# Three score tiles of 576 neighbouring PSUM columns, filled two tiles ahead

## The chip, the cores and the metric

The kernel runs on one core of one Trainium2 chip. The metric is the device time of one execution in microseconds (us). The core has TensorE (PE: matmuls, with PEld for its weight loads), VectorE (DVE), ScalarE (ACT), GpSimd (POOL), SyncE (SP), whose queue issues all loads, stores and DMA transposes here, and PSUM, the memory that PE writes its products to.

## The reference

Three stages follow one another. First attention with a top-k mask on q, k and v of shape 4 x 8 x 576 x 64:

```
scores = q @ k.T / sqrt(64)
kth = the 32nd largest score of each row
attn = exp(scores - max) where scores >= kth, else 0
attn = attn / (sum(attn) + 1e-9)
x = attn @ v          # heads side by side: 2304 tokens x 512
```

Then two two-layer networks on the 2304 tokens, 512 to 2048 to 512: the first with h * sigmoid(h) between its layers, the second with ELU (h where h > 0, else exp(h) - 1). All inputs are fp32.

## The kernel before

The work is cut into 18 chunks of 128 tokens and each chunk into 8 tiles, 144 tiles in all. A tile is one head's 128 query rows against all 576 keys. As 576 is 4 x 128 + 64, the 64 rows left over of two batches share one chunk, whose tiles hold two heads. The chunks come as batch 0 (4), leftovers of 0 and 1, batch 1 (4), batch 2 (4), leftovers of 2 and 3, batch 3 (4). Values are split into two fp16 halves (hi and lo) so that fp16 matmuls keep fp32 accuracy.

`slot(s)` writes out by hand the order of all instructions of one step of the pipeline; nothing is reordered afterwards, so each engine works through its queue in that order. In slot s stand:

- the scores of tile s+1 (`emit_qk`, L463): 4 matmuls of 288 columns, or 8 for two heads, after the mask of tile s-1, whose buffer they take;
- on DVE the top-k of tiles s and s-1, interleaved: four times MAX8 (the 8 largest of a row, L495) and three times MATCH_REPLACE8 (take them out, L499). The first of each reads the scores in PSUM, the later ones an SBUF copy `r`. After the first MATCH_REPLACE8 comes `bias` (L508), and ACT takes the exponential of the raw scores (L510). Last comes the mask (L523): keep the exponential where the score is at least the 32nd largest, and add the row up. Of tile s the slot holds the first four DVE steps, of tile s-1 the last four. In the order written, the exponential of tile s comes before the mask of tile s-1;
- `emit_ehi(s-1)` on ACT (L549), `emit_elo(s-2)` on POOL (L555, L556) and a DMA transpose into `et` (L558), then `emit_av(s-3)` on PE (L577): exponentials times values. There is one buffer `e16` between them;
- the two networks, 13 and 25 slots behind: `emit_in` (PE, 48 matmuls, L633), `emit_act` (ACT, 3 or 4 instructions), `emit_g` (POOL, L661), `emit_ghi` (ACT, L665), `emit_glo` (POOL), `emit_out` (PE, 12 matmuls of 512 columns, L681). A slot holds one such step. In slots whose number is 2 modulo 8 the attention output of a chunk is taken over (`emit_evac`, `x_hi`, `x_lo`); at the end of slots with 5 modulo 8 the input of the second network is scaled and split on ACT (`x_hi(1, ...)`: the `y` and `x` pieces), and POOL's half follows.

Queries, keys and values must be scaled and split before use. `prep` places these steps: the load, a sum of squares on ACT (`square`), for keys and values a matmul that adds the sums up over partitions (`add_up`, L175, into a spare column of the next score tile), a few one-column instructions on DVE, and the split: `*_hi` on ACT at the end of a slot, `*_lo` (a subtraction, L164) on POOL in the next. For batch 0 the keys come right before use; for batches 1 to 3 keys and values are prepared early, kept in DRAM and fetched later. A reduced sum stands at the end of slot r, its split at the end of slot r+2. Before, r is 17+4i for the keys of pair i of batch 1, 39+8i of batch 2, 73+8i of batch 3, and the values come 2, 4 and 4 slots after. Query sums stand at the end of even slots, query splits at the end of odd ones.

The decoding, scaling and splitting of the networks' weights (DVE, ACT, POOL) goes on through slots -3 to 24.

The score tiles before: two buffers `ps_s`, each of two banks of 512 columns, of which the first 288 hold half of the scores. So every tile has its banks to itself. The changed kernel has one tile object of four banks, and its three tiles of 576 columns follow one another without a gap.

Of the kernel before, what the change touches and what calls it, by code (L numbers as in the profile page):

```python
# [10 lines left out]
F32 = mybir.dt.float32  # L11
# [3 lines left out]
AF = mybir.ActivationFunctionType  # L15
ALU = mybir.AluOpType
AX = mybir.AxisListType.X
PSUM = bass.MemoryType.PSUM
# [13 lines left out]
def kernel(  # L32
# [11 lines left out]
    nc = tc.nc  # L44
    B, H, S, D = q.shape
# [6 lines left out]
    LO = S - SF  # L52
    KR = S // 64
    NC = FC + 1
    HALF = S // 2
    NWP = KFF
    NS = KFF // 4
    NP = H // 2
# [3 lines left out]
    def pool(name, bufs, **kw):  # L62
        return ctx.enter_context(tc.tile_pool(name=name, bufs=bufs, **kw))
# [22 lines left out]
    qs_p = pool("qs", 5)  # L86
    dram = pool("dram", 1, space=bass.MemoryType.DRAM)
    p2_p = pool("p2", 6)
    ps_s = pool("ps_s", 2, space=PSUM)
    ps_h = pool("ps_h", 2, space=PSUM)  # L90
    ps_a = pool("ps_a", 1, space=PSUM)
    ps_v = pool("ps_v", 1, space=PSUM)
# [13 lines left out]
    NTILE = NCH * H  # L106
# [5 lines left out]
    def tile_heads(t):  # L112
        kind, b, c = chunks[t // H]
        j = t % H
        if kind == "f":
            return [(b, j)]
        e, i = LEFT[j]
        return [(b + e, 2 * i), (b + e, 2 * i + 1)]
# [49 lines left out]
    fixed = const.tile([128, 2 + NXS], F32, name="fixed")  # L168
    g1, ones = fixed[:, 0:1], fixed.bitcast(BF16)[:, 2:3]
    due = []  # L170

    def add_up(ps):
        for x, (m, done) in enumerate(due):
            dst = ps[:, 1, HALF + 8 * x:HALF + 8 * x + 1]
            nc.tensor.matmul(out=dst, lhsT=ones.to_broadcast([128, 128]), rhs=m.bitcast(BF16)[:, 1:2], start=True, stop=True)  # L175
            done(dst)
        due.clear()
# [273 lines left out]
    Sps, ets, avs = {}, {}, {}  # L451
    rs_p = pool("rs", 2)

    def emit_qk(t):
        ps = ps_s.tile([128, 2, 512], F32, tag="S", name="S")
        qt = qT[t // 2]
        hs = tile_heads(t)
        n = 128 // len(hs)
        for e, bh in enumerate(hs):
            kt = kT[bh]  # L460
            for p in range(2):
                for a in range(2):
                    nc.tensor.matmul(  # L463
                        out=ps[n * e:n * e + n, a, 0:HALF],
                        lhsT=qt[:, 2 * (t % 2) + p, n * e:n * e + n],
                        rhs=kt[:, a * HALF:(a + 1) * HALF],
                        start=(p == 0),
                        stop=(p == 1),
                    )
        Sps[t] = ps  # L470

    e32s, sums, lsums, cs = {}, {}, {}, {}

# [6 lines left out]
        cs[t] = small.tile([128, 2], F32, tag="c", name="c")  # L480
        pmul(cs[t], qsc[t // 2][:, 2:3].to_broadcast([128, 2]), ik[:, b * NP + h // 2, :])

    def fold(x):
        return x.rearrange("p (a x) -> p a x", a=2)

    def topk_ops(t):
        st = {}
        n = TOPK // 8
        src = Sps[t][:, :, 0:HALF]

        def mx(i):
            if i == 0:
                st["m8"] = small.tile([128, n, 8], F32, tag="m8", name="m8")
                st["r"] = r_p.tile([128, S], F32, tag="r", name="r")
            nc.vector.max(st["m8"][:, i, :], src if i == 0 else st["r"])  # L495

        def mr(i):
            r = st["r"]
            nc.vector.match_replace(  # L499
                out=fold(r) if i == 0 else r,  # L500
                in_to_replace=st["m8"][:, i, :],
                in_values=src if i == 0 else r,
                imm_value=LOW,
            )
            if i == 0:
                c = cs[t]
                bias = small.tile([128, 1], F32, tag="bias", name="bias")
                nc.vector.tensor_scalar(bias, st["m8"][:, 0, 0:1], c[:, 1:2], LN2_14, op0=ALU.mult, op1=ALU.add)  # L508
                e = e32_p.tile([128, S], F32, tag="e32", name="e32")
                nc.scalar.activation(out=fold(e), in_=src, func=AF.Exp, scale=c[:, 0:1], bias=bias)  # L510
                e32s[t] = e

        def mask():
            e = fold(e32s[t])
            ch, j = divmod(t, H)
            if j == 0:
                sums[ch] = rs_p.tile([128, H], F32, tag="sum", name="sum")
                if chunks[ch][0] == "l":
                    lsums[ch] = rs_p.tile([128, H], F32, tag="lsum", name="lsum")
            if chunks[ch][0] == "l":  # L520
                j = LEFT[j][0] * NP + LEFT[j][1]
            acc = lsums.get(ch, sums[ch])[:, j:j + 1]
            nc.vector.scalar_tensor_tensor(  # L523
                e, src, st["m8"][:, n - 1, 7:8], e, op0=ALU.is_ge, op1=ALU.mult, accum_out=acc
            )
            Sps.pop(t)

        ops = []
        for i in range(n):
            ops.append(lambda i=i: mx(i))  # L530
            if i < n - 1:
                ops.append(lambda i=i: mr(i))
        ops.append(mask)
        return ops

# [11 lines left out]
    def emit_ehi(t):  # L547
        h = e16_p.tile([128, 2 * S], F16, tag="e16", name="e16")
        nc.scalar.activation(out=h[:, 0:S], in_=e32s[t], func=AF.Copy)  # L549
        e16s[t] = h  # L550
# [140 lines left out]
    def x2_copy(ch):  # L691
        acc = accs.pop((0, ch))
        y = o_p.tile([128, DM], F32, tag="o", name="y")
        nc.vector.tensor_scalar(y, acc, 1.0, None, op0=ALU.mult)
        z = small.tile([128, 4], F32, tag="z", name="z")
        square(y, z[:, 0:1])
        x2s[ch] = (y, z)
        return z[:, 0:1]
# [38 lines left out]

    KEARLY = 1  # L740
    LDA = -99
    LDB = 28
    LAG = 13
# [8 lines left out]
    loads, sumsq, tiny, early, splits, late, low, decs = (defaultdict(list) for _ in range(8))  # L752

    def prep(slots, load, total, reduce, ops, hi, lo):
        s0, s1, s2 = slots
        if reduce and s1 >= 0:
            s0, s1 = s0 - 1, s1 - 1
        loads[s0].append(load)

        def a():  # L760
            m = total()
            if reduce:
                due.append((m, lambda m: early[s2].append(lambda: ops(m=m))))
            else:
                tiny[s2].append(ops)

        sumsq[s1].append(a)
        late[s2].append((hi, lo))

    first = {b: min(t for (bb, _), t in first_use.items() if bb == b) for b in range(B)}  # L770
    for (b, i), t in first_use.items():
        x = dict(b=b, i=i)
        if b == 0:
            prep((t - 5, t - 4, t - 3), partial(k_load, **x), partial(k_sum, **x), True,
                 partial(k_ops, **x), partial(k_hi, **x), partial(k_lo, **x))
            late[t - 2].append((partial(k_tp, **x), None))
            prep((t - 1, t, t + 1), partial(v_load, **x), partial(v_sum, **x), True,
                 partial(v_ops, **x), partial(v_hi, **x), partial(v_lo, **x))
        else:
            d = 2 if b == 1 else 4  # L780
            r = first[b] - 17 - 8 * (d - 2) + 2 * d * i
            prep((r, r + 1, r + 2), partial(k_load, **x), partial(k_sum, **x), True,
                 partial(k_ops, **x), partial(k_hi, **x), partial(k_keep, **x))
            late[t - 3].append((partial(k_tp, **x), None))
            r += d
            prep((r, r + 1, r + 2), partial(v_load, **x), partial(v_sum, **x), True,
                 partial(v_ops, **x), partial(v_hi, **x, keep=True), partial(v_keep, **x))
            loads[t].append(partial(v_back, **x))
    for g in range(NTILE // 2):
        t = 2 * g  # L790
        prep((t - 5, t - 4, t - 3), partial(q_load, g), partial(q_sum, g), False,
             partial(q_ops, g), partial(q_hi, g), partial(q_lo, g))

    wload, wnow = defaultdict(list), defaultdict(list)
# [31 lines left out]
    for n in range(NWP):  # L826
        x = n, None
# [15 lines left out]
    def slot(s):  # L843
        cur, p1, p2, p5 = (mlp_step(s - x) for x in (0, 1, 2, 5))
        if 0 <= s < NTILE:
            tops[s] = topk_ops(s)
        a = tops.get(s, [])
        b = tops.pop(s - 1, [])
        if due and s < 0:
            add_up(ps_s.tile([128, 2, 512], F32, tag="S", name="S"))  # L850
        summed = [f() for f in early.pop(s, [])]
        small_ops = in_turn(summed + [f() for f in tiny.pop(s, [])])
        pieces = [w_dec_ops(*x, psum=2 <= s < LAG) for x in decs[s]]
# [5 lines left out]
        def dv(*qs, more=True):  # L859
            for o in qs:  # L860
                if o:
                    o.pop(0)()
                if small_ops and (more or s < 0):
                    small_ops.pop(0)()
                for _ in range(per):
                    if dec:
                        dec.pop(0)()
# [21 lines left out]
        if p3 and p3[2] == NS - 1:  # L889
            l, ch, i = p3  # L890
            if l == 0:
                z = x2_copy(ch)
# [12 lines left out]
        t = s - 3  # L905
# [12 lines left out]
        dv(b)  # L918
        if 0 <= s - 1 < NTILE:
            emit_ehi(s - 1)  # L920
        if 0 <= s + 1 < NTILE:
            emit_qk(s + 1)
        if due:
            add_up(Sps[s + 1] if 0 <= s + 1 < NTILE else ps_s.tile([128, 2, 512], F32, tag="S", name="S"))
        dv(a)
        small_ops += in_turn(f() for f in early.pop(s, []) + tiny.pop(s, []) + low[s])
        while small_ops or dec:
# [22 lines left out]
        if s % H == 0 and 0 <= s // H - 1 < NCH:  # L950
            kind, bb, c = chunks[s // H - 1]
# [38 lines left out]
```

## Time and profile before

| | us |
|---|---|
| median of 3 runs | 1188.23 (1186.55 to 1189.44) |
| profiled execution, first to last instruction (span) | 1185.1 |
| PE busy | 940.7 (79%) |
| DVE busy | 1017.0 (86%) |
| ACT busy | 851.7 (72%) |
| POOL busy | 832.6 (70%) |

The page gives no time for what lies around the span. The shares are averages over a first stage, up to about 200 us, in which weights are decoded beside the first tiles, a main stage, up to about 1075 us, in which attention and the networks overlap, and an end, in which only the networks are left. So the stages have to be read one by one.

### The profile page before, as it was taken

How to read it: one execution, taken by the hardware profiler on the slowest of the kernel's cores; microseconds unless marked ns; L12 is line 12 of the kernel's file. 1: busy time of each engine (PE TensorE's matmuls, PEld its weight loads, DVE VectorE, ACT ScalarE, POOL GpSimd, SP SyncE). 2: the span in 40 equal slices, each digit the busy share in tenths (PEclk: the TensorE clock that was granted, in tenths of full speed). 3: DMA queues.
4: the chain of work that ended last, by engine and by line, in shares of the span. 5: the costliest groups of instructions: out<-in, count | busy, mean ns of one | idle time of the engine just before them, and what ended most of it. 6: DMA issues, size and time to landing. Idle time of an engine off the chain costs nothing.

```text
span 1185.1 us, 30883 instructions
## 1 busy us (share of the span) xinstructions
PE 940.7 (79%) x11574; PEld 694.3 (59%) x11574; DVE 1017.0 (86%) x2595; ACT 851.7 (72%) x1663; POOL 832.6 (70%) x1070
## 2 busy tenths in 40 slices
PE   0011112657899999999999989999999999999997
PEld 0000102536666777677767667676777777777765
DVE  6999998997898899999999989999989999995000
ACT  5557556668877788788777778787767777776654
POOL 1148968599777778778776777777776776876543
PEclk9999999878999999999999999999999999999999
DMA  9967473354467646554456545454673444443100
GB/s 307 269 185 225 105 237 87 78 101 102 97 128 122 119 87 119 95 112 100 97 116 133 118 86 110 94 103 104 122 124 67 85 78 82 90 66 65 28 15 14
DMA packets 317318, 132.45 MB, mean 112 GB/s; under 512 B 293488, under 2 KB 300656, under 8 KB 317168
## 3 DMA queue, kind: packets, MB, share of 16 engines
q1 hardware_dynamic: 317168, 130.48, 50.6%
q8 instruction: 91, 1.49, 0.5%
q14 instruction: 59, 0.48, 0.2%
HBM read 52.17 MB, written 12.19 MB: 54 GB/s over the span
## 4 chain that ended last, share of the span: by engine, by line
PE 34%; DVE 20%; POOL 17%; DMA 11%; issue 11%; ACT 5%; SPq 2%; POOLq 0%; ACTq 0%; DVEq 0%
PE a L681 14%; PE h L633 14%; DVE m L495 5%; DMA et<-e 5%; DVE r L499 5%; POOL e L555 4%; POOL gh L164 3%; POOL t L661 3%; PE av L577 3%; PE S L463 3%; DVE W L265 2%; DVE h L262 2%; DVE h L258 2%; DMA W<-in_moe_w_in_dram 2%; DVE e L523 1%
## 5 line engine op out<-in xcount | busy, mean ns | idle before, releaser
L633 PE MATMUL h<-xt,W 128*128 128x128 f16 x6912 | 417.2, 221 | 2.0 <-DMA xt<-x 2.0
L633 PEld LDWEIGHTS <-W 128*128 128x128 f16 x6912 | 402.0, 99 | 14.8 <-issue 4.3
L681 PE MATMUL a<-W,gh 128*128 128x512 f16 x1728 | 401.3, 381 | 9.7 <-POOL gh L164 8.8
L495 DVE MAX8 m<-r 128x8 f32<-128x576 f32 x432 | 312.7, 749 | 1.2
L555 POOL TENSOR_TENSOR e<-e,e 128x512 f16<-128x512 f32 x144 | 167.1, 1160 | 171.5 <-ACT e L549 169.1
L681 PEld LDWEIGHTS <-gh 128*128 128x128 f16 x1728 | 158.9, 98 | 187.4 <-POOL gh L164 16.4
L463 PE MATMUL S<-kt,qt 128*128 128x288 f16 (+1 forms) x640 | 102.8, 304 | 183.4 <-DVE e L523 88.2
L164 POOL TENSOR_TENSOR gh<-t,gh 128x512 f16<-128x512 f32 x144 | 167.0, 1160 | 68.7 <-ACT gh L665 66.2
L499 DVE MATCH_REPLACE8 r<-m,r 128x576 f32<-128x576 f32 x288 | 213.9, 743 | 0.0
L661 POOL TENSOR_TENSOR t<-u,t 128x512 f32<-128x512 f32 x144 | 183.0, 1271 | 30.0 <-ACT u L655 24.6
L463 PEld LDWEIGHTS <-qt 128*128 128x128 f16 (+1 forms) x640 | 56.7, 103 | 241.0 <-issue 104.4
L665 ACT ACTIVATE gh<-t 128x512 f16<-128x512 f32 x144 | 90.2, 626 | 128.2 <-POOL t L661 127.8
L510 ACT ACTIVATE e<-S,bias,c 128x576 f32<-128x576 f32 x144 | 118.0, 819 | 55.6 <-DVE bias L508 50.1
L549 ACT ACTIVATE e<-e 128x576 f16<-128x576 f32 x144 | 97.4, 676 | 62.2 <-DVE p L133 19.1
L495 DVE MAX8 m<-S 128x8 f32<-128x576 f32 x144 | 109.0, 757 | 24.2 <-PE S L463 23.5
L577 PE MATMUL av<-vt,et 128*128 128x64 f16 (+1 forms) x2240 | 95.2, 198 | 26.2 <-DMA et<-e 25.8
L523 DVE SCALAR_TENSOR_TENSOR e<-S,m,e 128x576 f32<-128x576 f32 x144 | 115.4, 802 | 0.5 <-ACT e L510 0.4
L499 DVE MATCH_REPLACE8 r<-m,S 128x576 f32<-128x576 f32 x144 | 107.6, 747 | 0.0
L577 PEld LDWEIGHTS <-et 128*128 128x128 f16 (+1 forms) x2240 | 83.2, 104 | 34.4 <-DMA et<-e 31.4
L164 POOL TENSOR_TENSOR W<-W 128x512 f16<-128x512 f32 x64 | 74.0, 1156 | 5.4
L655 ACT ACTIVATE u<-u,c 128x512 f32<-128x512 f32 x72 | 58.6, 814 | 2.4
L652 ACT ACTIVATE u<-h,c 128x512 f32<-128x512 f32 x72 | 48.4, 673 | 12.4 <-PE h L633 12.4
(108 smaller groups left out, 1134.4 us busy)
## 6 DMA issues: line engine op xcount, KB each, us to landing
W<-in_moe_w_in_dram SPq DMA_DIRECT2D x32, 512.0 KB, 6.6
W<-in_moe_w_out_dram SPq DMA_DIRECT2D x25, 512.0 KB, 5.5
kn<-in_k_dram SPq DMA_DIRECT2D x16, 288.0 KB, 3.1
qn<-in_q_dram SPq DMA_DIRECT2D x64, 64.0 KB, 2.6
out_dram<-o SPq DMA_DIRECT2D x16, 256.0 KB, 2.7
vd<-v SPq DMA_DIRECT2D x12, 320.0 KB, 3.3
vt<-vd SPq DMA_DIRECT2D x24, 160.0 KB, 3.0
kd<-k SPq DMA_DIRECT2D x12, 288.0 KB, 2.2
```

The lines of the kernel that those rows point to most:

```text
L164: nc.gpsimd.tensor_tensor(dst, x, hi, op=ALU.subtract)
L463: nc.tensor.matmul(out=ps[n * e:n * e + n, a, 0:HALF], lhsT=qt[:, 2 * (t % 2) + p, n * e:n * e + n], rhs=kt[:, a * HALF:(a + 1) * HALF], s ...
L495: nc.vector.max(st["m8"][:, i, :], src if i == 0 else st["r"])
L499: nc.vector.match_replace(out=fold(r) if i == 0 else r, in_to_replace=st["m8"][:, i, :], in_values=src if i == 0 else r, imm_value=LOW,)
L510: nc.scalar.activation(out=fold(e), in_=src, func=AF.Exp, scale=c[:, 0:1], bias=bias)
L523: nc.vector.scalar_tensor_tensor(e, src, st["m8"][:, n - 1, 7:8], e, op0=ALU.is_ge, op1=ALU.mult, accum_out=acc)
L549: nc.scalar.activation(out=h[:, 0:S], in_=e32s[t], func=AF.Copy)
L555: nc.gpsimd.tensor_tensor(h[:, S + LO:2 * S], e[:, 0:SF], h[:, 0:SF], op=ALU.subtract)
L577: nc.tensor.matmul(out=o, lhsT=et[:, c, n * e:n * e + n], rhs=r, start=(i == 0), stop=(i == len(seq) - 1))
L633: nc.tensor.matmul(out=ps[:, f:f + 128], lhsT=w, rhs=xt[:, z, :], start=(kk == 0 and x == 0), stop=(kk == KDM - 1 and x == 2),)
L661: nc.gpsimd.tensor_tensor(t, u, t, op=ALU.add if l else ALU.mult)
L681: nc.tensor.matmul(out=acc, lhsT=gh[:, z, u * 128:(u + 1) * 128], rhs=W[:, n, w * 512:(w + 1) * 512], start=(m == 0 and x == 0), stop=(m = ...
```

## The change

One PSUM tile `scores` of four banks is made once. Tile t uses the 576 columns from 576 * (t mod 3); its matmuls are cut where a 512-column bank ends, as 512+64, 448+128 or 384+192. The spare columns of `add_up` come behind the three tiles, from 1728 on. The scores of tile s+2 are written in slot s, where those of s+1 were, after the mask of tile s-1 as before. Queries, and the keys of batch 0, are prepared one slot earlier. The later keys and values have r = 18+4i (batch 1), 37+8i (batch 2) and 73+8i (batch 3), and the keys are brought back one slot earlier (`k_tp`). Query sums then stand at the end of odd slots, query splits at the end of even ones. The first slot is -5 in place of -4. DVE and ACT read a flat run of 576 columns in place of two runs of 288.

```diff
-    ps_s = pool("ps_s", 2, space=PSUM)
+    ps_s = pool("ps_s", 1, space=PSUM)
...
-    def add_up(ps):
+    SB = 3
+    scores = ps_s.tile([128, 4 * 512], F32, name="S")
+
+    def add_up(s):
         for x, (m, done) in enumerate(due):
-            dst = ps[:, 1, HALF + 8 * x:HALF + 8 * x + 1]
+            y = SB * S + 128 * (s % 2) + 8 * x
+            dst = scores[:, y:y + 1]
...
     def emit_qk(t):
-        ps = ps_s.tile([128, 2, 512], F32, tag="S", name="S")
+        x0 = S * (t % SB)
+        cut = 512 * (x0 // 512 + 1) - x0
...
-                for a in range(2):
+                for a, z in ((0, cut), (cut, S)):
                     nc.tensor.matmul(
-                        out=ps[n * e:n * e + n, a, 0:HALF],
+                        out=scores[n * e:n * e + n, x0 + a:x0 + z],
                         lhsT=qt[:, 2 * (t % 2) + p, n * e:n * e + n],
-                        rhs=kt[:, a * HALF:(a + 1) * HALF],
+                        rhs=kt[:, a:z],
...
-        Sps[t] = ps
+        Sps[t] = scores[:, x0:x0 + S]
...
-        src = Sps[t][:, :, 0:HALF]
+        src = Sps[t]
...
-    KEARLY = 1
+    AHEAD = SB - 1
...
         if b == 0:
-            prep((t - 5, t - 4, t - 3), partial(k_load, **x), partial(k_sum, **x), True,
+            y = t - AHEAD
+            prep((y - 4, y - 3, y - 2), partial(k_load, **x), partial(k_sum, **x), True,
                  partial(k_ops, **x), partial(k_hi, **x), partial(k_lo, **x))
-            late[t - 2].append((partial(k_tp, **x), None))
+            late[y - 1].append((partial(k_tp, **x), None))
...
             d = 2 if b == 1 else 4
-            r = first[b] - 17 - 8 * (d - 2) + 2 * d * i
+            r = first[b] - 35 + 2 * d * i + (19 if b == 1 else 2 * (b % 2))
...
-            late[t - 3].append((partial(k_tp, **x), None))
+            late[t - AHEAD - 2].append((partial(k_tp, **x), None))
...
     for g in range(NTILE // 2):
-        t = 2 * g
-        prep((t - 5, t - 4, t - 3), partial(q_load, g), partial(q_sum, g), False,
+        t = 2 * g - AHEAD
+        prep((t - 4, t - 3, t - 2), partial(q_load, g), partial(q_sum, g), False,
...
-        if 0 <= s + 1 < NTILE:
-            emit_qk(s + 1)
+        if 0 <= s + AHEAD < NTILE:
+            emit_qk(s + AHEAD)
         if due:
-            add_up(Sps[s + 1] if 0 <= s + 1 < NTILE else ps_s.tile([128, 2, 512], F32, tag="S", name="S"))
+            add_up(s + 1)
```

## Rows read from the trace of the kernel before

**Rows 1.** Busy time by stretch: stretch, length, PE, PEld, DVE, ACT, POOL, clock, DMA.
```profile
0.00:30.00 30.00, 2.73 (x12) 1.52 (x12) 19.42 (x48) 15.98 (x42) 5.87 (x12) 1.00 0.93 307
...
226.00:290.00 64.00, 44.03 (x476) 31.47 (x472) 56.80 (x155) 45.72 (x89) 60.88 (x80) 0.81 0.46 94
290.00:440.00 150.00, 144.00 (x1834) 105.00 (x1831) 136.36 (x365) 117.91 (x229) 112.40 (x152) 0.99 0.59 115
440.00:665.00 225.00, 213.30 (x2681) 158.98 (x2679) 213.69 (x564) 179.02 (x346) 168.89 (x217) 1.00 0.55 108
665.00:840.00 175.00, 165.16 (x2079) 121.80 (x2077) 163.18 (x430) 139.76 (x270) 131.09 (x171) 1.00 0.52 104
840.00:1075.00 235.00, 235.00 (x3022) 176.11 (x3019) 228.87 (x579) 179.65 (x336) 173.74 (x229) 1.00 0.48 87
```

**Rows 2.** Order of time, PE, around 570 us: start, length, instructions merged.
```profile
567.81 0.65 PE L463 MATMUL S<-kt,qt 128*128 128x288 f16 x4
568.30 2.84 PE L633 MATMUL h<-xt,W 128*128 128x128 f16 x48
570.98 0.57 PE L577 MATMUL av<-vt,et 128*128 128x64 f16 x14
571.39 2.75 PE L681 MATMUL a<-W,gh 128*128 128x512 f16 x12
573.98 0.65 PE L463 MATMUL S<-kt,qt 128*128 128x288 f16 x4
```

**Rows 3.** Waits from 290 to 840 us: who, for whom: us, times, longest.
```profile
ACT gh L665 <- POOL t L661: 67.4, 44, 2.3
...
PE av L577 <- DMA et<-e: 19.6, 17, 3.0
DVE m L495 <- PE S L463: 14.5, 18, 2.0
```

**Rows 4.** Order of time, DVE, from 755 to 762 us.
```profile
756.04 0.77 DVE L495 MAX8 m<-S 128x8 f32<-128x576 f32 x1 [0.20 <-PE S L463]
...
758.18 0.20 DVE L508 TENSOR_SCALAR bias<-m,c 128x1 f32<-128x1 f32 x1
758.30 1.41 DVE L495 MAX8 m<-r 128x8 f32<-128x576 f32 x2
759.63 0.80 DVE L523 SCALAR_TENSOR_TENSOR e<-S,m,e 128x576 f32<-128x576 f32 x1
```

**Rows 5.** Order of time, ACT, before the exponential of tile 94.
```profile
762.15 0.74 ACT L158 ACTIVATE sq<-vn 128x640 fp8e4<-128x640 f32 x1 [0.86 <-DMA vn<-in_v_dram]
...
762.88 0.39 ACT L161 ACTIVATE qn<-qn,qs 128x128 f32<-128x128 f32 x1
763.30 0.42 ACT L440 ACTIVATE q<-qn 128x256 f16<-128x256 f32 x1
763.62 0.70 ACT L161 ACTIVATE y<-y,z 128x512 f32<-128x512 f32 x1
764.36 0.63 ACT L602 ACTIVATE x<-y 128x512 f16<-128x512 f32 x1
764.90 0.81 ACT L510 ACTIVATE e<-S,bias,c 128x576 f32<-128x576 f32 x1
```

**Rows 6.** Order of time, ACT, around the exponential of tile 26.
```profile
302.74 0.81 ACT L161 ACTIVATE vn<-vn,sv 128x640 f32<-128x640 f32 x1
303.59 0.74 ACT L411 ACTIVATE v<-vn 128x640 f16<-128x640 f32 x1
...
304.97 0.81 ACT L510 ACTIVATE e<-S,bias,c 128x576 f32<-128x576 f32 x1
```

**Rows 7.** Order of time, DVE: the mask of tile 25.
```profile
303.61 0.81 DVE L523 SCALAR_TENSOR_TENSOR e<-S,m,e 128x576 f32<-128x576 f32 x1
```

**Rows 8.** Order of time, ACT: the exponential of tile 142.
```profile
1070.22 0.81 ACT L510 ACTIVATE e<-S,bias,c 128x576 f32<-128x576 f32 x1
```

**Rows 9.** Order of time, DVE: the mask of tile 141.
```profile
1069.71 0.80 DVE L523 SCALAR_TENSOR_TENSOR e<-S,m,e 128x576 f32<-128x576 f32 x1
```

More of the change, by code (lines that the diff above doesn't have):

```diff
@@ L54 @@
     NC = FC + 1
-    HALF = S // 2
     NWP = KFF
@@ L481, in emit_c @@
         pmul(cs[t], qsc[t // 2][:, 2:3].to_broadcast([128, 2]), ik[:, b * NP + h // 2, :])
-    def fold(x):
-        return x.rearrange("p (a x) -> p a x", a=2)
     def topk_ops(t):
@@ L499, in mr @@
             nc.vector.match_replace(
-                out=fold(r) if i == 0 else r,
+                out=r,
                 in_to_replace=st["m8"][:, i, :],
@@ L509, in mr @@
                 e = e32_p.tile([128, S], F32, tag="e32", name="e32")
-                nc.scalar.activation(out=fold(e), in_=src, func=AF.Exp, scale=c[:, 0:1], bias=bias)
+                nc.scalar.activation(out=e, in_=src, func=AF.Exp, scale=c[:, 0:1], bias=bias)
                 e32s[t] = e
         def mask():
-            e = fold(e32s[t])
+            e = e32s[t]
             ch, j = divmod(t, H)
@@ L849, in slot @@
         if due and s < 0:
-            add_up(ps_s.tile([128, 2, 512], F32, tag="S", name="S"))
+            add_up(s)
         summed = [f() for f in early.pop(s, [])]
```

## The prediction

> **What bounds the kernel now.** I first read busy time by stretch [rows 1]. Up to 30 us VectorE (DVE) works 19.4 us and waits for the first loads. From 226 to 290 us GpSimd (POOL) is the full engine, 60.9 of 64 us. From 290 us on, TensorE (PE) leads: it is idle for 150 - 144.0 = 6.0, 225 - 213.3 = 11.7 and 175 - 165.2 = 9.8 us, 27.5 us together up to 840 us, and for nothing from 840 to 1075 us. DVE is close behind: 36.8 us idle from 290 to 840, 6.1 us from 840 to 1075.
>
> Next, the order of time of PE around 570 us [rows 2]: from one score group to the next, 567.81 to 573.98, is 6.17 us with nothing idle. That is the least a slot of the main stage can take. From 290 to 840 us there are 84 slots, 6.5 us each, so the whole stage could give back at most the 27.5 us, and the stage after 840 us nothing.
>
> Then the waits of 290 to 840 us [rows 3]. PE stands still mainly because `et`, the transposed exponentials, is late (19.6 us in 17 waits). That chain is mask (DVE), `emit_ehi` (ScalarE, ACT), `emit_elo` (POOL), DMA, `emit_av` (PE). DVE waits for scores 14.5 us in 18 waits. But PE idles little beside it, so those DVE waits are mostly DVE keeping pace with PE. ACT waits 67.4 us in 44 waits for POOL before `gh`, 1.5 us each, which is slack that a later exponential may use.
>
> Last, one slot in detail [rows 4, 5]. The bias of tile 94 ends at 758.38, yet ACT takes its exponential at 764.90, because before it stand a sum of squares of `vn`, the `qn`/`q` pieces and the `y`/`x` pieces of the end of slot 93. DVE ran the mask of tile 93 at 759.63 meanwhile. So DVE is ahead of ACT here by over 5 us.
>
> **The change part by part.**
>
> *Two tiles ahead.* The scores of tile s+2 go where tile s-1 lay, so their matmuls stand at the same place of PE's queue and wait for the same mask(s-1) as those of s+1 do now. What is new is that the scores are wanted one slot later. This removes at most DVE's 14.5 us of waits. While PE is the fuller engine, DVE then only runs ahead and waits elsewhere. Ends: 0 and -14.5; I take 0, since PE's queue sets the slot.
>
> *Pieces of 512+64, 448+128, 384+192 for 288+288.* Same 576 columns, same count of matmuls. The `av` group does 14 matmuls of 64 columns, each with weights of its own, in 571.39 - 570.98 = 0.41 us, 29 ns each [rows 2], so a short piece costs its columns and the edit is 0. The other end: a short piece costs as much as 288 columns do, 0.12 us; beside 512 columns at 2.59 / 12 = 0.216 us this is 2 x 0.336 - 0.49 = 0.18 us a tile, 0.18 x 119 = +21 us after 290 us. Below zero is excluded by the equal columns. I take 0, the row of that size. Flat instead of folded reads by DVE: 0.77 us from the score tile against 1.41 / 2 = 0.70 from a flat tile [rows 4], at most -0.07 a read, on an engine that isn't first: 0.
>
> *Neighbouring columns.* Tiles 0 and 1 of the three now lie together in the columns 512 to 1023, tiles 1 and 2 in 1024 to 1535. Until now every tile had its 512-column banks to itself, so no row shows whether order inside one tile object is kept by column or by bank. If by column, nothing is added. If by bank, two waits come:
> 1. mask(s-1) on DVE waits for exponential(s) on ACT when s mod 3 is 1 or 2. Queued behind the mask on DVE are the rest of top-k(s), all of tile s+1, and on PE the scores of s+2.
> 2. The first max of s+1 waits for the scores of s+2 in two of three slots, at the very place where it waits for PE today, so the first edit's gain shrinks to a third.
>
> I take the bank. In these sentences alone the Trainium skill is weighed: "PSUM — Partial Sum Buffer", section "PSUM bank collisions raise a hardware error", says that no two of TensorE, ScalarE and VectorE may be in one bank and 32-partition quadrant at one time, two readers included, so each such pair has to be ordered. By it the second wait list holds and the term below is paid; by columns alone it would be 0. No row of this trace shows it.
>
> Price of wait 1: how far the exponential's end lies behind the mask's start, for tiles 25 to 143 with s mod 3 not 0, from 305.78 - 303.61 = 2.17 us [rows 6, 7] to 1071.03 - 1069.71 = 1.3 us [rows 8, 9], 57 of 80 tiles above zero, sum 113 us. That is the far end (+113, every wait paid anew). But DVE needs to fall behind only once: after that the exponentials of ordinary slots lie before the mask by themselves. What can be paid again is the rise from one slot to the next beyond the 1.5 us that ACT spends waiting for POOL. Over tiles 25 to 105 that is 16 rises, 25 us in all; from tile 106 on next to nothing (0.2 us), because no key or value is prepared there. Part of the 25 lands where PE would idle for `et` anyway. I take +8, with the next edit counted in.
>
> *Preparation shifted.* Query pieces leave the odd slots' ends for the even ones. Those of batch 2 go from slots 39, 41, 43, 45 + 8i (key sum, key split, value sum, value split) to 37, 39, 41, 43; batch 1 moves one slot later, batch 3 stays. Before, the end of slot 5 of 8 in batch 2 held the value split (304.33 - 302.74 = 1.59 us, [rows 6]), the query split (763.62 - 762.88 = 0.74) and the `y`/`x` pieces (764.90 - 763.62 = 1.28) [rows 5]: 3.6 us before one exponential. After, it holds a key sum (about the 0.73 us of the `vn` one), a query sum (0.4, estimated from the 0.39 of `qn`) and `y`/`x`: 2.4 us. POOL's query subtraction likewise leaves the slots in which it subtracts `x`. The slots in which `et` comes late get lighter in all three batches. Nothing is added in work or DMAs; the SP queue issues the same loads one slot apart. Ends: 0 and all 27.5 us of PE's idle time; a negative effect is possible where batch 1 still meets the query split (4 keys, 4 values, 0.74 us each: +6). I take half of the idle time, -13: the heaviest end of slot loses 1.2 of its 3.6 us, and the pieces that stay still come before an exponential.
>
> *Start.* One more slot of loads, and tile 0 is prepared before the first weights land. DVE has 30 - 19.4 = 10.6 us idle there [rows 1]. Loads of four weights now stand behind the first key transposes in the SP queue. Ends -4 and +4; I take -1. The stage up to 226 us is filled by the same DVE work. From 226 to 290 us POOL's sum stays but for one key's subtraction that leaves it (-1.4 at best); I take 0.
>
> Sum: 0 + 0 + 8 - 13 - 1 = -6 us on the span of 1185.1 us, 1179 us. The page gives no time around that span; the three timed runs lie 1.5 to 4.3 us above it, their median 3.1, and I carry that over: 1182 us.
>
> **The rivals.**
> *Bank waits decide (slower).* DVE stops at mask(s-1) for the exponential of the heavy slots, PE stops behind it at the scores of s+2, and ACT's next exponential then waits for DVE's bias. For it: DVE is only 37 us of 550 short of full, so what it loses it can't make up, and the overlap goes to 6 us in single slots. Against: the lead need be given up only once. If the 25 us of rises are paid in full and half as much returns in the slots after them, with the lighter slots giving back 13 of it, the sum is about 25 + 12 - 13 - 1 = +23. The case lies between 0 and that, its middle at 1188 + 12 = 1200. It decides once the rises are worth over 14 us.
> *Nothing nets.* Waits added and slots lightened cancel, or `et` is late through its DMA, which is unmoved: 1188 us.
> *Columns only, DVE freed.* No wait is added and DVE may run a slot ahead: -13, and up to 6 more of the idle time: 1188 - 18 = 1170. That the change then frees more is barred by PE's 6.17 us.
>
> **How the numbers follow.** Forecast 45%, bank waits decide 30%, nothing nets 18%, columns only 7%. 0.2% is 2.4 us, about what can be told from no change. Faster: 43 of the 45 (the rest within 2.4 us) and 7, 50%; within: 18 and 2, less 1 that falls on the slower side, 19%; slower: 31%. The forecast's own range is 1174 to 1187. The range for 8 in 10 reaches from the columns-only case, 1166, past the middle of the slower case to 1203.
>
> **What would show it.** Right: PE idle 290 to 840 us about 14 us less for `et`; "DVE e <- ACT e" (mask waiting for the exponential) as a new wait, of some tens of us at most, in two of three slots; exponentials starting within 0.1 us of their bias more often. Wrong: no such wait (columns), then a shorter time; or PE's score group waiting for the mask by several us in slots 4 and 6 of 8, then a longer one; or PE's slot longer than 6.17 us from 840 us on, which would be the price of the short pieces.

## The result and the profile after

The changed kernel takes 1200.83 us (median of 4 runs, 1200.39 to 1202.79) against 1187.39 us for the kernel before in the same series: ratio 1.0122, 95% interval 1.0105 to 1.0139. It is 1.2% slower. The profiled execution's span is 1199.1 us, 14.0 us more than before.

Busy time by stretch of the changed kernel, with the columns of [rows 1]:

```profile
226.00:290.00 64.00, 43.34 (x481) 30.77 (x480) 57.32 (x155) 46.23 (x90) 61.88 (x82) 0.84 0.46 96
290.00:440.00 150.00, 139.04 (x1786) 101.46 (x1784) 131.52 (x354) 117.76 (x227) 110.88 (x150) 0.99 0.59 114
440.00:665.00 225.00, 210.77 (x2619) 154.37 (x2618) 208.78 (x551) 179.61 (x343) 167.09 (x215) 0.99 0.55 106
665.00:840.00 175.00, 162.32 (x2014) 119.41 (x2012) 158.82 (x423) 136.32 (x260) 127.48 (x163) 0.98 0.50 100
840.00:1075.00 235.00, 232.80 (x2972) 170.04 (x2971) 225.15 (x568) 174.25 (x328) 168.03 (x223) 1.00 0.49 87
```

PE is now idle for 11.0, 14.2 and 12.7 us in the three stretches from 290 to 840 us, 37.9 us together against 27.5 [rows 1], and for 2.2 us after 840, where it was never idle. DVE idles more too: 50.9 us against 36.8. So no engine has taken PE's place; the engines wait for each other more.

The waits of the changed kernel from 290 to 840 us, with the columns of [rows 3]:

```profile
DVE e L523 <- ACT e L510: 44.5, 25, 4.2
ACT e L510 <- DVE bias L508: 42.9, 42, 2.2
PE S L466 <- DVE e L523: 37.5, 34, 3.8
ACT gh L665 <- POOL t L661: 21.7, 29, 1.8
ACT sq L157 <- DMA vn<-in_v_dram: 17.0, 9, 3.1
ACT sq L157 <- DMA qn<-in_q_dram: 9.8, 11, 1.8
...
DVE m L495 <- PE S L466: 3.6, 6, 1.4
...
PE av L577 <- DMA et<-e: 0.3, 1, 0.3
```

PE's waits for `et` are gone (19.6 us before [rows 3]), and so is most of DVE's waiting for scores (14.5). Both are outweighed by a new chain: the mask waits for the exponential of the next tile (44.5 us), and the next scores wait for that mask (37.5). ACT now often waits for DVE's `bias` (42.9 us in 42 waits, against 4.0 in 4 before), which it did not need to while DVE ran ahead.

One such place in full. The order of time of ACT before the exponential of tile 86 (715.39), with the idle time before a row and what ended it in brackets:

```profile
709.60 0.68 ACT L549 ACTIVATE e<-e 128x576 f16<-128x576 f32 x1
712.95 0.74 ACT L157 ACTIVATE sq<-vn 128x640 fp8e4<-128x640 f32 x1 [2.67 <-DMA vn<-in_v_dram]
713.59 0.19 ACT L157 ACTIVATION_READ_ACCUMULATOR sq<-vn 128x1 f32 x1
713.81 0.31 ACT L157 ACTIVATE sq<-qn 128x128 fp8e4<-128x128 f32 x1
...
714.11 0.70 ACT L160 ACTIVATE y<-y,z 128x512 f32<-128x512 f32 x1
714.85 0.63 ACT L602 ACTIVATE x<-y 128x512 f16<-128x512 f32 x1
715.39 0.81 ACT L510 ACTIVATE e<-S,bias,c 128x576 f32<-128x576 f32 x1
```

The same on DVE: the bias of tile 86, and the mask of tile 85 at 716.23:

```profile
710.97 0.21 DVE L508 TENSOR_SCALAR bias<-m,c 128x1 f32<-128x1 f32 x1
711.09 1.42 DVE L495 MAX8 m<-r 128x8 f32<-128x576 f32 x2
716.23 0.82 DVE L523 SCALAR_TENSOR_TENSOR e<-S,m,e 128x576 f32<-128x576 f32 x1 [3.73 <-ACT e L510]
```

And on PE: the scores of tile 87 (cut 512+64) and of tile 88 (448+128):

```profile
707.57 0.65 PE L466 MATMUL S<-kt,qt 128*128 128x512 f16 x4
708.05 2.84 PE L633 MATMUL h<-xt,W 128*128 128x128 f16 x48
...
711.14 2.75 PE L681 MATMUL a<-W,gh 128*128 128x512 f16 x12
717.11 0.65 PE L466 MATMUL S<-kt,qt 128*128 128x448 f16 x4 [3.21 <-DVE e L523]
717.60 0.17 PE L177 MATMUL S<-mv,fixed 128*128 128x1 bf16 x1
717.63 2.84 PE L633 MATMUL h<-xt,W 128*128 128x128 f16 x48
```

The bias of tile 86 ends at 711.18, so its exponential needs nothing more from then on. But in ACT's queue a sum of squares stands ahead of it, and ACT stands idle for 2.67 us until the values for that sum have arrived. Behind that sum stand a query's, the `y` and `x` pieces, then the exponential, 4.2 us after the bias. DVE's mask of tile 85 waits 3.73 us for it, PE's scores of tile 88 wait 3.21 us for the mask. Before, DVE wrote that mask without looking at the exponential [rows 4, 5]. The score groups themselves take 708.05 - 707.57 = 0.48 and 717.60 - 717.11 = 0.49 us; 288+288 took 0.49 [rows 2].

The mask of tile 77, DVE in order of time, shows the same wait at a tile for which the prediction expected none, since 78 mod 3 is 0 and the tiles 77 and 78 have no bank in common:

```profile
660.42 0.82 DVE L523 SCALAR_TENSOR_TENSOR e<-S,m,e 128x576 f32<-128x576 f32 x1 [3.79 <-ACT e L510]
```

SP's queue ahead of that stall at 712.95 (SPq rows are issues, not transfers):

```profile
705.93 1.29 SPq L558 DMA_TRANSPOSE et<-e  x1
707.27 0.63 SPq L318 DMA_DIRECT2D vn<-in_v_dram  x1
...
709.25 0.59 SPq L328 DMA_DIRECT2D qn<-in_q_dram  x1
```

The loads stand behind the transpose that is issued in their slot, and are issued one after the other; the sums that need them are at the end of the same slot (712.95 and 713.81).

### The profile page after: what moved, and what is told of

It reads as the page before. It is cut to its first block, busy times and chain, and to the rows that moved or that the text cites. A ratio compares the mean times of both kernels' runs of the same rounds, so it can differ in the third digit from the quotient of the medians.

```text
span 1199.1 us, 30805 instructions
## 1 busy us (share of the span) xinstructions
PE 943.3 (79%) x11574; PEld 687.7 (57%) x11574; DVE 1016.0 (85%) x2595; ACT 857.0 (71%) x1663; POOL 833.6 (70%) x1070
## 4 chain that ended last, share of the span: by engine, by line
POOL 23%; DVE 21%; PE 16%; issue 16%; DMA 14%; ACT 7%; SPq 3%; POOLq 0%; ACTq 0%; DVEq 0%
PE h L633 8%; DMA et<-e 6%; PE a L681 6%; POOL t L661 6%; DVE m L495 5%; POOL e L555 5%; DVE r L499 5%; POOL gh L163 4%; DVE e L523 2%; DVE W L267 2%; DVE h L264 2%; DVE h L260 2%; DMA qn<-in_q_dram 2%; POOL e L556 2%; DMA W<-in_moe_w_in_dram 2%
## 5 line engine op out<-in xcount | busy, mean ns | idle before, releaser
L633 PE MATMUL h<-xt,W 128*128 128x128 f16 x6912 | 421.7, 223 | 2.0 <-DMA xt<-x 2.0
L466 PE MATMUL S<-kt,qt 128*128 128x512 f16 (+10 forms) x640 | 103.7, 305 | 229.4 <-DVE e L523 211.6
L466 PEld LDWEIGHTS <-qt 128*128 128x128 f16 (+1 forms) x640 | 52.7, 104 | 294.2 <-issue 232.9
L549 ACT ACTIVATE e<-e 128x576 f16<-128x576 f32 x144 | 97.5, 677 | 69.0 <-DMA et<-e 20.6
```

The lines of the kernel that those rows point to most:

```text
L466: nc.tensor.matmul(out=scores[n * e:n * e + n, x0 + a:x0 + z], lhsT=qt[:, 2 * (t % 2) + p, n * e:n * e + n], rhs=kt[:, a:z], start=(p == 0 ...
L633: nc.tensor.matmul(out=ps[:, f:f + 128], lhsT=w, rhs=xt[:, z, :], start=(kk == 0 and x == 0), stop=(kk == KDM - 1 and x == 2),)
```

## The experiments

All ratios are to the kernel before on the same chip, five rounds, with the 95% interval. Two new orders are at stake, the places of the preparation and the order in the score tiles, and each was tried alone. "Loads early" below means that `prep`'s loads from slot 14 on are issued one slot earlier, and nothing else.

**The preparation alone, on the kernel before** (two banks a tile, one tile ahead; the diff has its core, and batch 0's keys and `k_tp` move one slot earlier too).

```diff
-            r = first[b] - 17 - 8 * (d - 2) + 2 * d * i
+            r = first[b] - 35 + 2 * d * i + (19 if b == 1 else 2 * (b % 2))
...
-        prep((t - 5, t - 4, t - 3), partial(q_load, g), partial(q_sum, g), False,
+        prep((t - 6, t - 5, t - 4), partial(q_load, g), partial(q_sum, g), False,
```

> The kernel before with only the new places of preparation (queries and batch-0 keys one slot earlier, batches 1 to 3 as changed, keys brought back one slot earlier); two score tiles with banks of their own, scores one tile ahead. Theory 1 (the mask's new wait for the next tile's exponential costs, the lighter slots give back): ratio to before 0.99 to 0.998, no wait of the mask for ScalarE, TensorE's waits for et down from 20 us to under 10. Theory 2 (the shifted preparation itself costs): 1.008 to 1.015. Theory 3 (the two-ahead scores and cut matmuls cost): 0.998 to 1.002.

Measured 1.0116 (1.0097 to 1.0134), inside the range of theory 2. On the kernel before, the new places cost 13.8 us where the prediction had them give 13. But this is not quite the term of the change: with scores one tile ahead a key tile is here held one slot longer, while in the changed kernel its scores come a slot earlier too.

**The order alone**: both score tiles of the kernel before in one tile object, each with its own two banks as before.

```diff
+    both = ps_s.tile([128, 2, 2, 512], F32, name="S")
...
-        ps = ps_s.tile([128, 2, 512], F32, tag="S", name="S")
+        ps = both[:, t % 2]
```

> The kernel before, with its two score tiles made as one tile object of four banks; each tile keeps its own two banks, nothing else changes. It adds only the order between the exponential of tile s and the mask of tile s-1, in every slot. Theory 1: slower, 1.010 to 1.025, since the heavy slots are the old ones; the mask waits over 40 us in all for ScalarE. Theories 2 and 3: 0.998 to 1.003.

Measured 1.0101 (1.0085 to 1.0117), 12 us. Its waits from 290 to 840 us:

```profile
DVE e L524 <- ACT e L511: 39.6, 22, 4.8
PE S L464 <- DVE e L524: 29.3, 26, 4.2
```

No two tiles share a bank here, yet the mask waits for the next tile's exponential. So two tiles of one object are ordered even where they have no bank in common. In the changed kernel that order does not stop at the slots with a shared bank either, as the row at 660.42 shows.

Part of this price is paid in TensorE's clock. From the mask of tile 24 to that of tile 104, with the columns of [rows 1], the kernel before and then one object:

```profile
296.85:833.59 536.74, 509.66 (x6423) 376.42 (x6421) 501.57 (x1326) 425.77 (x819) 401.95 (x523) 1.00 0.55 108
297.10:844.90 547.80, 516.35 (x6420) 383.69 (x6418) 500.27 (x1326) 429.72 (x823) 403.16 (x523) 0.98 0.53 107
```

Of the 11.1 us by which this stretch is longer, PE stands idle for 4.4, and 6.7 go to its matmuls, as many as before, at a mean granted clock of 0.98 in place of 1.00. The longest stall shows how:

```profile
664.50 1.12 PE L464 MATMUL S<-kt,qt 128*128 128x288 f16 x4 [4.23 <-DVE e L524]
665.48 4.91 PE L634 MATMUL h<-xt,W 128*128 128x128 f16 x48
```

Behind it 48 matmuls take 4.91 us, against 2.84 in [rows 2]; from 665 to 670 us the granted clock is 0.51, the lower of its two levels (1.2 GHz). In the changed kernel the same stretch has 10.4 us more of idle PE and 2.4 us more of matmuls than in the kernel before.

**Both together, on the kernel before.**

> Both edits of the two runs above together: one tile object of four banks and the new places of preparation, scores still one tile ahead, matmuls still 288 and 288. Theory 1: within 0.3% of the changed kernel, 1.009 to 1.015. Theory 2: the same 1.008 to 1.015, but then one_object alone is at 1.000. Theory 3: 1.000.

Measured 1.0245 (1.0225 to 1.0264), above both ranges: the two losses add up, 1.0116 x 1.0101 = 1.0218, and a little more. The changed kernel is 1.2% better than this.

**The exponential written later in the changed kernel**, behind `emit_ehi(s-1)`, meant to put the mask ahead of it.

```diff
-                nc.scalar.activation(out=e, in_=src, func=AF.Exp, scale=c[:, 0:1], bias=bias)
+                exps[t] = lambda: nc.scalar.activation(out=e, in_=src, func=AF.Exp, scale=c[:, 0:1], bias=bias)
...
+        if s in exps:
+            exps.pop(s)()
```

> The changed kernel with the exponential of tile s written behind the mask and the fp16 copy of tile s-1, so that the mask never waits for it; instead the first max of s+1 and the scores of s+2 wait for it. Theory 1: most of the 55 us of mask waits go and return in part as waits of TensorE and of the first max: 0.995 to 1.006. Theories 2 and 3: 1.010 to 1.014, as the changed kernel.

Measured 1.0737 (1.0718 to 1.0757), a miss of every expectation. The mask's wait went, but the one object orders other pairs in the score tiles as well. From 290 to 840 us:

```profile
PE S L466 <- ACT e L510: 60.7, 73, 2.5
DVE m L495 <- PE S L466: 24.9, 26, 1.6
```

The scores two tiles on now wait for the later exponential, and the first max of the next tile for those scores.

**The new places without the keys' earlier return, and split in two**: all new places of queries and later keys and values (qr_same_ktp), the keys' and values' alone (r_only), the queries' alone (q_only). Their edits are the lines of the first diff.

> The kernel before with queries prepared one slot earlier and the changed places of batches 1 to 3, but the keys brought back where they were, so that no key tile is held a slot longer. If the 1.2% of prep_only came from holding key tiles longer (a ninth buffer of nine in the leftover chunks): 0.996 to 1.003. If the shifted places themselves cost: 1.008 to 1.013. If the lighter slots give what was forecast: 0.985 to 0.992.

> The kernel before with the changed places of keys and values of batches 1 to 3 alone; their loads stay apart from the queries' in batches 2 and 3 and leave the query slots' neighbours in batch 1. If meeting loads are the cause: 0.997 to 1.003. If the places of keys and values were what cost in qr_same_ktp: 1.004 to 1.009.

> The kernel before with queries alone prepared one slot earlier: their loads move from even slots to odd ones, where the loads of the later keys and values stand too. If loads that meet in one slot hold ScalarE's sums and with them the slot: 1.003 to 1.009, ScalarE's waits for loads up from 29 us to 35 to 45. If the new places of keys and values were what cost in qr_same_ktp: 0.997 to 1.002.

Measured 1.0068 (1.0047 to 1.0088), 1.0005 (0.9992 to 1.0017) and 1.0103 (1.0081 to 1.0126). So the queries' shift costs the 1%, the other places are free, and the two together cost 0.7%, which lies in none of the three ranges for it. In batch 1 the new places of r_only bring key and value loads into the queries' slots (both even), so loads in one slot do not cost by that alone. The first experiment's other 0.5% goes with what it had besides: the keys brought back a slot earlier, or batch 0's keys prepared a slot earlier. No run parts these two. From 290 to 840 us, with the queries shifted alone:

```profile
DVE p L133 <- ACT sq L158: 32.6, 15, 4.6
...
PE av L577 <- DMA et<-e: 27.6, 20, 5.4
```

and one of those waits in order of time, the sum of a value on ACT and then DVE:

```profile
767.64 0.74 ACT L158 ACTIVATE sq<-vn 128x640 fp8e4<-128x640 f32 x1 [0.96 <-DMA vn<-in_v_dram]
...
768.93 0.15 DVE L133 TENSOR_SCALAR p<-qs 128x1 int32<-128x1 int32 x1 [2.65 <-ACT sq L158]
```

The one-column instruction `p` stands in DVE's queue ahead of the rest of the top-k and waits for ACT's sum of the query. That sum stands behind the value's, which had waited 0.96 us for its load and takes 0.74 itself; the fp16 copy ahead of both (L549) had waited 1.43 us for a transpose, so the load is about 1 of the 2.65 us. So even where no mask waits for ACT, a late load stops DVE.

**The changed kernel with the old `r`.**

> The changed kernel with the places of keys and values of batches 1 to 3 as before; queries and the two-ahead scores stay changed. If the new places lighten the slots: slower than the changed kernel, 1.015 to 1.022. If they cost: 1.000 to 1.008. If they do nothing: 1.010 to 1.014.

Measured 1.0164 (1.0142 to 1.0185), in the range for places that lighten the slots: going back makes it worse by 0.4%. The new `r` is not what is wrong.

**Loads early**, in the changed kernel, in the kernel before, in qr_same_ktp and in one_object:

```diff
-        loads[s0].append(load)
+        loads[s0 - 1 if s0 >= 14 else s0].append(load)
```

> The changed kernel with the loads of keys, values and queries issued one slot earlier from slot 14 on; nothing else. ScalarE's waits for the value load (about 21 us, at the end of the slot whose next exponential the mask waits 3.7 to 4.1 us for) should go. If the mask's wait takes its length from what ScalarE does and waits for before the exponential: 1.003 to 1.009, mask waits under 45 us. If the order alone costs, whatever its length: 1.011 to 1.014.

> The kernel before with the same earlier loads. There the mask doesn't wait for ScalarE, so only et comes earlier: 0.993 to 1.000. If the same share goes as in the changed kernel (the loads cost by themselves): 0.990 to 0.995.

> qr_same_ktp with all loads one slot earlier from slot 14 on. If its 0.7% is ScalarE waiting for loads: 0.986 to 0.993, level with or below the kernel before with the same earlier loads (0.991). If it is the order of the work itself: 0.997 to 1.001.

> one_object (the mask's new wait alone, old places) with all loads one slot earlier. If the wait's price is ScalarE held by loads before the exponential: 0.991 to 0.997. If the order costs by itself, with the sums and splits alone: 1.000 to 1.005.

| | loads as they were | loads early |
|---|---|---|
| kernel before | 1 | 0.991 (0.9894 to 0.9926) |
| new places, keys' return as before | 1.0068 | **0.981 (0.979 to 0.9829)** |
| one object | 1.0101 | 0.9968 (0.9953 to 0.9984) |
| changed kernel | 1.0122 | 0.991 (0.9897 to 0.9923) |

With the loads early the sign of the new places turns: 0.981 / 0.991 = 0.990, a gain of 1.0% or 12 us. The one object then costs 0.9968 / 0.991, 0.6% in place of 1.0%. The changed kernel gains 2.1% and comes out below both of its ranges; the kernel before gains 0.9%, in its second range; the new places with early loads come out below both of theirs. The best version is the kernel before with the new places and early loads: 1163.59 us, faster than both kernels. Its busy time, columns as in [rows 1]:

```profile
290.00:840.00 550.00, 536.43 (x6812) 397.60 (x6809) 526.65 (x1396) 452.50 (x869) 425.49 (x557) 1.00 0.58 112
840.00:1075.00 235.00, 234.24 (x2992) 175.92 (x2991) 215.13 (x538) 173.32 (x323) 170.98 (x221) 1.00 0.45 81
```

PE idles 13.6 us from 290 to 840 us, against 27.5 before [rows 1] and 37.9 in the changed kernel. The waits of the changed kernel with early loads, same stretch:

```profile
DVE e L523 <- ACT e L510: 21.6, 22, 2.8
PE S L466 <- DVE e L523: 17.4, 32, 2.4
```

The new chain is halved, not gone. No sum waits for a load any more, so what stays is put down to ACT's own work ahead of the exponential.

**Query load and sum ahead of the key's or value's in their slot**, with the queries' shift alone and in the changed kernel:

```diff
-        loads[s0].append(load)
+        loads[s0].insert(len(loads[s0]) if reduce else 0, load)
```

(and the same for `sumsq[s1]`).

> q_only with the query's load and its sum of squares ahead of the key's or value's where both stand in one slot. If the 1.0% of q_only is VectorE waiting for a query sum queued behind a value sum that waits for its load: 0.995 to 1.003, VectorE's waits for the sums under 12 us (32.6 in q_only). If it is the loads meeting in the DMA queues: 1.007 to 1.012.

> The changed kernel with the same: query loads and sums first. Here the exponential, too, stands behind the value sum, and the mask waits for it, so taking the query out of that queue alone should give less: 1.006 to 1.012. If the query queue was the whole loss: 0.995 to 1.001. If the meeting loads: 1.011 to 1.014.

Measured 1.0099 (1.0082 to 1.0117) and 1.0123 (1.0105 to 1.014), no change: the place inside the slot is not it. Both lie in the ranges for loads that meet in the DMA queues, but the transfers themselves are hardly slower: a query load of 64 KB takes 2.6 us from issue to landing (median, 290 to 1075 us) in the kernel before and 2.8 with the queries shifted, a value load of 160 KB 3.2 and 3.5. From 290 to 1075 us of the first:

```profile
DVE p L133 <- PE S L175: 14.0, 12, 3.6
...
DVE p L133 <- ACT sq L158: 10.4, 8, 2.9
```

DVE's wait for query sums fell from 32.6 to 10.4 us, but the key and value sums are now behind, and DVE's wait for them (by way of PE's matmul of L175) rose from 4.2 to 14.0. PE's waits for `et` fell only from 31.2 to 24.9 us. Which load is late changed; that one of them is late did not.

**One kind of load early**: keys and values alone (`reduce and s0 >= 14`), queries alone (`not reduce and s0 >= 14`), each in the changed kernel and with the queries' shift alone.

> The changed kernel with the key and value loads of slots from 14 on issued one slot earlier, and the query loads left where they are. Theory A (ScalarE is held by the key and value loads, the 2.67 us before the vn sum, and everything behind it): most of the gain of all loads early (0.991 to the kernel before) stands, 0.992 to 0.997. Theory B (it is the query loads, which the change put into the slots of the key and value loads): 1.005 to 1.012.

> The changed kernel with the query loads alone one slot earlier. Theory A (key and value loads hold ScalarE): 1.008 to 1.014, the sums of the values still wait for their loads some 17 us in all. Theory B (query loads): 0.992 to 1.000.

> The kernel before with the query preparation one slot earlier, and the key and value loads alone one slot earlier. Theory A (key and value loads hold ScalarE where the query sums stand behind them): the loss of 1.0% goes and the gain of early loads comes, 0.985 to 0.995. Theory B (query loads): 1.003 to 1.010.

> The kernel before with the query preparation one slot earlier and its loads one slot earlier still; keys and values as before. Theory A: the loss stays, 1.006 to 1.011. Theory B: the loss goes, 0.995 to 1.002.

Measured 0.996 (0.9945 to 0.9975) and 1.0044 (1.0027 to 1.0062) in the changed kernel, 0.9927 (0.991 to 0.9944) and 0.9956 (0.994 to 0.9972) with the queries' shift alone. Neither theory holds by itself: two runs fall in a range of A, one in a range of B, and 1.0044 in neither. Both kinds of load hold ACT: in the changed kernel the keys' and values' loads alone give back 1.6% and the queries' alone 0.8%, all together 2.1%; with the queries' shift alone either move takes the whole loss away. Set beside ACT's waits for loads (the three rows `ACT sq <- DMA` of 290 to 1075 us added up):

| | waits of ACT for loads, us | ratio |
|---|---|---|
| kernel before | 29.1 | 1 |
| queries shifted | 36.2 | 1.0103 |
| ... query first in its slot | 36.1 | 1.0099 |
| ... query loads early | 19.7 | 0.9956 |
| ... key and value loads early | 16.8 | 0.9927 |
| queries and later keys and values shifted | 36.1 | 1.0068 |
| changed kernel | 36.6 | 1.0122 |
| ... query first in its slot | 31.4 | 1.0123 |
| ... old `r` | 31.3 | 1.0164 |
| ... query loads early | 18.4 | 1.0044 |
| ... key and value loads early | 17.8 | 0.996 |
| ... all early | 0 | 0.991 |

Each of these waits is from one profiled execution, whose time lies up to 0.6% from the median. Within each family the time falls where these waits are cut by about half or more. Smaller differences do not show in it: at 31.4 us the changed kernel is no faster than at 36.6, and at 31.3, with the old `r`, slower. Which load waits, and what stands behind it, matters too: at 18.4 and 17.8 us the changed kernel's two differ by 0.8%.

## Why the prediction was wrong

It was wrong in sign: 1182 us and a gain were forecast, 1200.83 and a loss measured. The range held the time, and the rival "bank waits decide" gave this number, 1200. Its chain is the one in the rows above: the mask waits for the exponential, the next scores for the mask, the next exponential for the bias. But in its sum the lighter slots give back 13 us, and they cost 8, while the waits cost 12 and not its 37. That its number came out is in part luck.

*The step that failed* is the shifted preparation, and in it the sentence "Nothing is added in work or DMAs; the SP queue issues the same loads one slot apart." The term was -13. The new places without the keys' return measured +0.68% of 1187 us, +8. With no load late the same places give -12 us, the forecast's size, and PE's waits for `et` from 290 to 1075 us fall from 19.8 us (kernel before, loads early) to 12.6, the forecast's way; so what was said of ACT's work holds up. But the loads were counted and not followed in time: the price of their new place was put at nothing. The shift puts query loads and sums into the slots of the key and value loads, behind the transpose and each other; ACT's waits for loads rise from 29.1 to 36.1 us, and what is behind them in ACT's queue waits too; so does the `p` in DVE's, 24.2 us for query sums against 6.0 before. A row for it was there: [rows 5] shows ACT waiting 0.86 us for `vn`, and the prediction counted the sum's 0.73 us and not the wait.

*Order in the score tiles*: +8 was forecast, +12 is what the order alone cost before the change (1.0101). The kind of wait was right and its size near. The reason was not: tiles of one object are ordered without a shared bank too, so the wait can come in every slot. The sentence that the lead "need be given up only once" held in part: the changed kernel has 29 such waits in the 119 slots from 290 to 1075 us, where the far end had 57 in 80, but the long ones (3.79 us for tile 77, 3.73 for tile 85) come back every eight slots, where a value's load, a query's sum and the `y`/`x` pieces meet. Two things were left out of the term. One is PE's clock behind a long stall, 6.7 us of it in the run with one object. The other is the end: the prediction has 0.2 us from tile 106 on, but from the mask of tile 116 to the end of the span the kernel before takes 269.8 us and the changed one 272.6 (one object 272.1), though no key or value is prepared there. Masks still wait there, 3.6 us in 5 waits from 950 to 1100 us; whether that is all of it no run shows.

*Two tiles ahead*: 0 was forecast. The losses of the order and of the new places multiply to 1.0101 x 1.0068 = 1.0170; the changed kernel's 1.0122 is 0.5% under that. With early loads the same product, 0.9968 / 0.991 x 0.981 = 0.987, is 0.4% under the measured 0.991. So the remainder (two tiles ahead, cut pieces, layout, the keys' return) is some half per cent, of either sign: no run isolated it, and its sign stays open. Against both losses together on the kernel before (1.0245) the changed kernel is 1.2% better, but there key tiles are held a slot longer. DVE's wait for scores fell from 14.5 to 3.6 us; with one object and scores still one tile ahead it fell to 6.2, so most of this is DVE being held by ACT instead. Where a wait for scores is left, it can be for those two tiles ahead, here the first max of tile 80 for the scores of tile 81:

```profile
670.35 0.65 PE L466 MATMUL S<-kt,qt 128*128 128x512 f16 x4
671.04 0.77 DVE L495 MAX8 m<-S 128x8 f32<-128x576 f32 x1 [1.42 <-PE S L466]
```

Tile 80's own scores had been written a slot before. Tiles 80 and 81 have no bank in common, so again it is the one object that orders them; a DVE that is level with PE gains nothing by the second tile.

*Cut pieces*: 0, as the rows of PE show (0.48 and 0.49 us against 0.49). *Start*: -1 was forecast; the first max of tile 24 starts 2.5 us earlier than before, within the bound of -4. The stretch from 290 to 840 us holds 82 slots of 6.7 us, not 84 of 6.5; nothing else hangs on that count.

*What was named as a sign* came in part: PE's waits for `et` fell by 19.3 us, but the time went to the score group that waits for the mask, with the longest waits in slots 6 of 8, which the prediction had named as the sign of a longer time.

*The sum*: +12 for the order and +8 for the places were measured, each on the kernel before; about -6 is what is left for the rest, to make the 14 us.

## What to carry to other kernels

Where one in-order engine stands between a load and two others, a step that is moved can lose by when its load lands what it gains by its work: read the engine's waits for DMA at the new place first, and issue the load a slot earlier (0.9% here for one line, and it turned the shift from +0.7% to -1.0%). Keep buffers that different engines use at one time in tile objects of their own: here the two tiles of one object were ordered without a shared bank. When a wait goes (`et`, 19.6 us), add up the engine's idle time over all that it waits for: PE idled 37.9 us in place of 27.5.

## What the runs showed that was not expected

Order by tile object. The Trainium skill, "PSUM — Partial Sum Buffer", section "PSUM bank collisions raise a hardware error", asks for order between engines by bank and 32-partition quadrant. The run with one object and separate banks shows an order wider than that, kept by the program as built and not by the memory: 39.6 us of masks waiting for exponentials in other banks, 1.0% of the time.

One slot of lead for loads. In the kernel before, sums waited for their loads 25 times between 290 and 1075 us, 2.6 us at most and 29.1 in all; issuing the loads a slot earlier was worth 0.9%. With all loads a slot earlier no sum waits for a load from 290 to 1075 us in any of the four kernels so changed.
